# A kernel of attention and two expert layers: the squares of the last three row blocks behind the last score turn's rounding, and half of the put products behind the last rank

## The chip, the cores and the metric

The kernel runs on one core of a Trainium2 chip. The metric is device time in microseconds (us) of one execution. The engines are TensorE (PE, matrix products), VectorE (DVE), ScalarE (ACT), GpSimd (POOL) and SyncE (SP, which issues transfers). Each engine executes its own queue in the order in which the program gives it. An instruction that waits for another engine holds up everything behind it on its own.

## What is computed

Attention with hashed buckets runs over 2 x 8 heads, 768 positions, 64 columns. Its output, 1,536 rows of 512 columns, goes through two layers of eight experts each: the first sends every row to one expert, the second to two.

```python
def _attn_ref(q, k, v, proj):
    ...
    mask = q_bucket[:, :, :, None] == k_bucket[:, :, None, :]
    scores = np.where(mask, scale * np.matmul(q, k.transpose(0, 1, 3, 2)), -1e9)
    attn = np.exp(scores - np.max(scores, axis=-1, keepdims=True))
    ...
def _moe_ref(x, expert_emb, tau, w1, w2):
    xn = x / (np.linalg.norm(x, axis=-1, keepdims=True) + 1e-06)
    logits = xn @ en.T / tau
    expert_idx = np.argmax(logits, axis=1)
    probs = np.exp(logits - logits.max(-1, keepdims=True))
    ...
    h = np.maximum(x[mask] @ w1[e], 0.0)
    out[mask] = gate_w[mask, None] * (h @ w2[e])
```

The change touches the norm of the rows (`np.linalg.norm`), whose sum of squares ACT computes, and the order around it.

## The kernel before

**Stages.** Attention fills 0 to about 287 us of the trace, the first expert layer about 287 to 493, the second the rest. Products in full precision are split into a high and a low part (names ending in `h` and `l`).

**Attention.** There are 32 groups `g` (16 heads, two halves of the rows), each with three score turns `j`. A turn is: PE's scores (L597), DVE's maximum (L602), the scale of it `mxs` (L607, L608, mostly on POOL), ACT's exponential (L612). Six transposes per group follow (L620), each rounded on ACT (`eh`, L624) with its rest on DVE (`el`, L630), and the products with the values (L647, L648). A group ends with ACT's copy `os` (L652), PE's L657 and DVE's L671 and L673, which write the rows `xrow` (task `fo`).

**Routing.** The 1,536 rows lie in twelve blocks of 128, taken in four triples T0 = 0, 3, 6, 9. For each triple there are, in the names of the planner's tasks:
- `rsa`, three squares of the first 448 columns, and `rsb`, three of the last 64 (function `r1_sq`, L679 to L684, the instruction is at L683). Each adds up its squares with an accumulator read right behind it.
- `r7` and `rm`, the logits and the best expert `hot` on DVE (L692 to L695, L686 to L690); `rr0` and `rr`, the rank of every row among those of its expert on PE (L241, L243, then L249, L251).
- `rn`, the norm on POOL (L304 to L306); `rv`, its application (L309, L310); `re`, the exponential of the gate on ACT (L313); `rg`, the gate (L317 to L319).
- `rp`, the row's place (L264, L267); `ra`, three scatters from POOL to memory (L719); `ro`, the overflow arithmetic on POOL (L274 to L279); `rc`, the carry of the rank to the next triple (L255, L257).

**The first expert** doesn't read its rows back. For T0 = 6 and 9 they are put into place by products (`xo`, `x0_put`, L769) of the rounded rows (`xa` on ACT, L756, and their rest `xb` on POOL, L759) with one-hot tiles (`oh`, DVE, L741). The products for the columns d = 0, 1 go to a tile S, those for d = 2, 3 to a tile ET. ACT and DVE copy both to `xh` (L1036) and `xl` (L1043), and the expert's first product starts (L1056). In the experts, `hh` and `hl` (L1062, L1066) are the hidden rows, L1080 to L1082 the second product, `ys` (L1104) its copy on ACT, L1125 its transpose. Weights come by SP (L202), are split on ACT (L211) and DVE (L217), and stand in ACT's queue between these. The second expert's rows and their weights `meta` come back from memory by SP (L996, L991), after the scatters, with the weights behind them in SP's queue.

**What sets the order.** The routines are tasks of a list scheduler, `Plan`. `add(name, engine, duration, function, due, dependencies, use=, new=)` registers one. `plan.order()` sorts all tasks by the starts that it plans from durations, due times and dependencies, and the instructions are emitted in that order, so that a planned duration of one task can move any task on any engine. `use` and `new` name ring slots: `new` opens one, here `("rt", T0)`, the small tiles of a triple. The first scatter of T0 = 6 depends also on `("rn", 9)`, so that all six scatters of the last two triples stand behind the norm of the last one on POOL.

Of the kernel before, what the change touches and what calls it, by code (L numbers as in the profile page):

```python
# [9 lines left out]
F32 = mybir.dt.float32  # L10
# [11 lines left out]
N, D, E, F = NB * S, NHEAD * DH, 8, 1024  # L22
# [33 lines left out]
class Plan:  # L56
# [7 lines left out]
    def add(self, name, eng, dur, fn, due, deps=(), use=(), new=(), lat=0):  # L64
        self.steps[name] = (eng, dur, fn, due, tuple(deps), tuple(use) + tuple(new), tuple(new), lat)
# [66 lines left out]
def lsh_attention_moe_moe2_kernel(  # L132
# [252 lines left out]
    acon, rt, rows = ap("acon", 1), ap("rt", 2), ap("rows", 1)  # L385
# [291 lines left out]
    R1 = {}  # L677

    def r1_sq(T0, t, last):  # L679
        if t == 0 and not last:  # L680
            R1[T0] = dict(ss=rt.tile([128, 3, 2], F32, name="ss"))
        c = slice(D - DH, D) if last else slice(0, D - DH)
        nc.scalar.activation(sqj[:, c], xrow[:, T0 + t, c], AF.Square,  # L683
                             accum_out=R1[T0]["ss"][:, t, last:last + 1])  # L684
# [6 lines left out]

    def r1_pre(T0):  # L692

        l7 = R1[T0]["l7"] = rt.tile([128, 3, E], F32, name="l7")
        nc.vector.tensor_reduce(l7, LGP[:, T0:T0 + 3, :, :NHEAD - 1], axis=AX.X, op=OP.add)  # L695

    def r1_hot(T0):
# [81 lines left out]
    add = plan.add  # L779
    P = lambda f, *a, **k: (lambda: f(*a, **k))  # L780
# [5 lines left out]
    for h in range(HEADS):  # L786
        z = 12 * h
        due = lambda k, o=0.0: z + PR[k] + o
        if h > 1:
            add(("load", h), "SP", 1800, P(loads, h), due("load"), [("load", h - 1)] if h > 2 else [], lat=2200,  # L790
                new=[("qk", h), ("vr", h)])
# [117 lines left out]
    for i, g in enumerate((14, 15, 30, 31)):  # L909
        T0, z = 3 * i, 6.0 * g + 8.5 + (L1 if i < 2 else 0)  # L910
        zg = z if i < 2 else z + 8 if i == 2 else z + 4
        hot = [("fo", x) for x in range(g % 2 + 16 * (g // 16), g + 1, 2)]
        w = L2 if i < 2 else .1
        prev = [("rc", T0 - 3)] if T0 else []
        for t in range(3):
            add(("rsa", T0, t), "ACT", 560, P(r1_sq, T0, t, 0), z - 3 + w * t, hot[:-1] + ([("rsa", T0, t - 1)] if t else []),
                use=[("rt", T0)] if t else [], new=[] if t else [("rt", T0)])
            add(("rsb", T0, t), "ACT", 240, P(r1_sq, T0, t, 1), z + (w * t if i < 2 else 4), hot + [("rsa", T0, 2)] + [("th", 31, 5)] * (i == 2), use=[("rt", T0)])
        U = dict(use=[("rt", T0)])
        add(("r7", T0), "DVE", 260, P(r1_pre, T0), z - 3, hot[:-1] + [("rsa", T0, 0)], use=[("rt", T0)])  # L920
        add(("rm", T0), "DVE", 760, P(r1_top, T0), 191.5 if i == 2 else z, hot + [("r7", T0)], use=[("rt", T0)])
        add(("rr0", T0), "PE", 120, P(r1_rank0, T0), z - (0 if i < 2 else 1), prev + [("tr", 31, 5)] * (i == 2) + [("c3",), ("rm", T0) if i < 2 else ("fp", g)], new=[("ET", ("k", T0))])
        add(("rr", T0), "PE", 228, P(r1_rank, T0), z, [("rm", T0), ("rr0", T0)], use=[("ET", ("k", T0)), ("rt", T0)])
        add(("rq", T0), "DVE", 452, P(r1_hot, T0), zg, [("rm", T0)] + [("tl", 1, 31, 5)] * (i == 2), **U)
        add(("rp", T0), "DVE", 315, P(r1_pos, T0), zg, [("rr", T0), ("rq", T0)],
            use=[("ET", ("k", T0)), ("rt", T0)])
        add(("rn", T0), "POOL", 1325, P(lambda T0: gate1_norm(rt, R1[T0]["ss"], 3, R1[T0]), T0), zg,
            [("rsb", T0, t) for t in range(3)], **U)
        add(("rv", T0), "DVE", 309, P(lambda T0: gate1_scale(3, R1[T0]), T0), zg, [("rn", T0), ("rm", T0)], **U)
        add(("re", T0), "ACT", 113, P(lambda T0: gate1_exp(R1[T0]), T0), zg, [("rv", T0)], **U)  # L930
        add(("rg", T0), "DVE", 506, P(lambda T0: gate1_out(rt, 3, R1[T0], xrow[:, T0:T0 + 3, D]), T0), zg,
            [("re", T0)] + [("fo", 31)] * (i == 2), **U)
        for t in range(3):
            add(("ra", T0, t), "POOL", 1038, P(r1_scatter, T0, t), z + 1 + w * t, [("rp", T0), ("rg", T0)]
                + ([("ra", T0, t - 1)] if t else []) + [("in", len(inits) - 1)]
                + ([("rn", 9)] if (T0, t) == (6, RA) else []), **U)
        if i < 3:
            add(("rc", T0), "POOL", 699, P(lambda T0: rank_carry(rt, R1[T0]["hot"], 3, 1), T0), z + (0 if i < 3 else 2),
                [("rm", T0), ("rr0", T0)] + prev, **U)
        add(("ro", T0), "POOL", 1064, P(r1_over, T0), z + 9, [("rp", T0), ("ra", 9 if i > 1 else T0, 2)], **U)  # L940
        add(("rk", T0), "SP", 1500, P(r1_keep, T0), z + (3 if i < 3 else 0), hot)
# [5 lines left out]
    for i, T0 in enumerate((6, 9)):  # L947
# [13 lines left out]
                use=[("ET", ("k", T0)), ("rt", T0)] + ([("es", ("oh", T0))] if t else []), new=[] if t else [("es", ("oh", T0))])  # L961
        for d in range(4):
            add(("xo", T0, d), "PE", 650, P(x0_put, T0, d), z + 1.5 + 3 * (d // 2) + d * .1 if i else 197 + 2 * (d // 2) + .1 * d,
                [("xb", T0, d), ("oh", T0, 2), ("e0t", d)] + ([("xo", 6, d)] if i else [("fp", 31)]),
                use=[(("S", "x0"), ("ET", "x0"))[d // 2], ("es", ("oh", T0))])
    for f in plan.order():
        f()
# [641 lines left out]
```

## Time and profile before

| | |
|---|---|
| time before, median of 3 runs | 811.01 us (807.99 to 813.76) |
| profiled execution | 808.55 us, span 806.8 us |
| mean granted clock of TensorE | 0.991 of full speed |
| PE busy | 774.3 us (96%) |
| DVE busy | 583.6 us (72%) |
| ACT busy | 479.5 us (59%) |
| POOL busy | 382.3 us (47%) |

A row of a timeline gives the start in us from the start of the span, the length, the engine, the line of the kernel, the operation, the tile written and the tiles read, the shapes, and in square brackets how long the engine stood idle ahead of it and what ended that. PE is busy nearly all the time, so the stretches in which it isn't, and what is waited for there, are what to look at.

### The profile page before, as it was taken

Reading aid. Unit: us, or ns where it says so; the run is one execution under the profiler, and the core shown is the slowest. Engines: PE = TensorE matmul, PEld = TensorE weight load, DVE = VectorE, ACT = ScalarE, POOL = GpSimd, SP = SyncE. Lnnn points to the kernel's source line nnn. Section 1 sums busy time; section 2 is a strip of 40 time slices with the busy share of each in tenths; the row PEclk is TensorE's granted clock in tenths of the full one; section 3 lists DMA queues with packets and bytes.
Section 4 is the critical chain, followed back from the end, with each engine's and each line's share of the span. In section 5 each row is a group of like instructions: output and inputs, shape, how many; then the busy total and the mean of one; then the engine's idle time right before and its main releaser. Section 6 shows DMA issues by size and latency. Waiting matters only on the chain. (4 is left out here: it accounts for less than half of the span.)

```text
span 806.8 us, 14991 instructions
## 1 busy us (share of the span) xinstructions
PE 774.3 (96%) x5078; PEld 748.5 (93%) x5078; DVE 583.6 (72%) x1303; ACT 479.5 (59%) x1009; POOL 382.3 (47%) x669
## 2 busy tenths in 40 slices
PE   8999798998999999999999998999999999999995
PEld 6899787987999999999999998999999999999995
DVE  8999778999999868887787756684566475665511
ACT  6997777986888847556575544464353435354310
POOL 6655344557464260433123322108373745648474
PEclk9999989999999999999999999999999999999998
DMA  8999999664322158886677645765786776856332
GB/s 215 290 237 233 244 235 247 208 187 143 112 67 53 46 178 252 258 255 196 207 231 218 214 161 176 183 192 93 195 172 173 171 182 132 177 147 118 85 35 80
DMA packets 94076, 141.16 MB, mean 175 GB/s; under 512 B 26220, under 2 KB 58116, under 8 KB 93994
## 3 DMA queue, kind: packets, MB, share of 16 engines
q1 hardware_dynamic: 76730, 123.45, 55.2%
q0 software_dynamic: 17264, 16.70, 11.1%
q8 instruction: 42, 0.69, 0.4%
q14 instruction: 40, 0.33, 0.1%
HBM read 89.08 MB, written 36.06 MB: 155 GB/s over the span
## 5 line engine op out<-in xcount | busy, mean ns | idle before, releaser
L1264 POOL DMA_INDIRECT out_dram<-yo,idx x91 | 147.6, 1622 | 127.6 <-DVE yo L1261 102.0
L1056 PE MATMUL S<-xh,w0h 128*128 128x256 f32 (+1 forms) x512 | 165.0, 322 | 1.0 <-DVE hl L1066 1.0
L1057 PE MATMUL S<-xl,w0h 128*128 128x256 f32 (+1 forms) x512 | 161.4, 315 | 0.3 <-issue 0.3
L1058 PE MATMUL S<-xh,w0l 128*128 128x256 f32 (+1 forms) x512 | 161.7, 316 | 0.0
L1080 PE MATMUL ET<-hh,w1h 128*128 128x256 f32 (+2 forms) x504 | 158.5, 315 | 0.1
L1082 PE MATMUL ET<-hh,w1l 128*128 128x256 f32 (+2 forms) x504 | 158.2, 314 | 0.0
L1081 PE MATMUL ET<-hl,w1h 128*128 128x256 f32 (+2 forms) x504 | 157.8, 313 | 0.0
L1062 ACT ACTIVATE hh<-S 128x512 fp32r<-128x512 f32 (+1 forms) x64 | 46.8, 732 | 136.1 <-PE S L1058 130.1
L630 DVE TENSOR_TENSOR el<-ET,eh 128x384 fp32r<-128x384 f32 x192 | 102.0, 551 | 16.1 <-ACT eh L624 13.9
L612 ACT ACTIVATE es<-S,mxs 128x768 f32<-128x768 f32 x96 | 95.5, 995 | 15.7 <-POOL mxs L608 12.8
L620 PE MATMUL ET<-idf,es 128*128 128x128 f32 x576 | 92.1, 277 | 9.7 <-ACT es L612 7.1
L1066 DVE SCALAR_TENSOR_TENSOR hl<-S,hh 128x512 fp32r<-128x512 f32 (+1 forms) x64 | 54.5, 852 | 64.2 <-ACT hh L1062 62.3
L624 ACT ACTIVATE eh<-ET 128x384 fp32r<-128x384 f32 x192 | 89.7, 492 | 14.6 <-PE ET L620 11.3
L1056 PEld LDWEIGHTS S<-xh,w0h 128*128 128x128 f32 x512 | 96.3, 188 | 1.4 <-DVE hl L1066 1.2
L1057 PEld LDWEIGHTS S<-xl,w0h 128*128 128x128 f32 x512 | 96.4, 188 | 1.3 <-issue 0.5
L1058 PEld LDWEIGHTS S<-xh,w0l 128*128 128x128 f32 x512 | 96.2, 188 | 0.3
L1080 PEld LDWEIGHTS ET<-hh,w1h 128*128 128x128 f32 x504 | 94.9, 188 | 1.1 <-ACT ys L1104 0.7
L1081 PEld LDWEIGHTS ET<-hl,w1h 128*128 128x128 f32 x504 | 94.8, 188 | 0.7
L602 DVE TENSOR_REDUCE mxs<-S 128x1 f32<-128x768 f32 x96 | 91.5, 953 | 5.1 <-PE S L597 4.0
L1082 PEld LDWEIGHTS ET<-hh,w1l 128*128 128x128 f32 x504 | 94.7, 188 | 0.3
L620 PEld LDWEIGHTS ET<-idf,es 128*128 128x128 f32 x576 | 71.9, 142 | 20.6 <-ACT es L612 8.1
L217 DVE TENSOR_TENSOR w1l<-wraw,w1h 128x512 fp32r<-128x512 f32 x128 | 81.9, 681 | 11.8 <-ACT w1h L211 11.8
(257 smaller groups left out, 1474.7 us busy)
## 6 DMA issues: line engine op xcount, KB each, us to landing
wraw<-in_w1a_dram SPq DMA_DIRECT2D x32, 512.0 KB
wraw<-in_w2a_dram SPq DMA_DIRECT2D x32, 512.0 KB
wraw<-in_w1b_dram SPq DMA_DIRECT2D x32, 512.0 KB
wraw<-in_w2b_dram SPq DMA_DIRECT2D x32, 512.0 KB
xs<-zrow SPq DMA_DIRECT2D x26, 260.5 KB
xr<-xs SPq DMA_DIRECT2D x28, 208.0 KB
qk<-in_qk_dram SPq DMA_DIRECT2D x15, 384.0 KB
xs<-zrow SPq DMA_DIRECT2D x16, 261.0 KB
```

Of the source, the lines that this page charges most:

```text
L602: nc.vector.tensor_reduce(MX[(3 * g + j) % 9][:, 0:1], SC[g, j][:, :, :384], axis=AX.XY, op=OP.max, negate=True)
L612: nc.scalar.activation(ES[g, j].rearrange("p (a b) -> p a b", a=2), SC[g, j][:, :, :384], AF.Exp, bias=mx[:, 2:3], scale=mx[:, 1:2], accum ...
L620: nc.tensor.transpose(T[:, j * 128:j * 128 + 128], ES[g, j][:, kb * 128:kb * 128 + 128], idf)
L624: nc.scalar.activation(EH[g, kb], ET[g, kb], AF.Copy)
L630: nc.vector.tensor_tensor(EL[g, kb], ET[g, kb], EH[g, kb], op=OP.subtract)
L1056: nc.tensor.matmul(o, wH[n][:, fs], xh, start=kd == 0, stop=False)
L1057: nc.tensor.matmul(o, wH[n][:, fs], xl, start=False, stop=False)
L1058: nc.tensor.matmul(o, wL[n][:, fs], xh, start=False, stop=kd == 3)
L1080: nc.tensor.matmul(P, wH[n][:, ws], hh, start=f == 0, stop=False)
L1081: nc.tensor.matmul(P, wH[n][:, ws], hl_, start=False, stop=False)
L1082: nc.tensor.matmul(P, wL[n][:, ws], hh, start=False, stop=f == 7)
L1264: s = nc.gpsimd.indirect_dma_start(out=out.rearrange("n (a c) -> (n a) c", a=4), out_offset=bass.IndirectOffsetOnAxis(ap=IDX[e][:, b:b + 1 ...
```

## The change

Planned durations of all squares go from 560 and 240 to 850 and 370. The long squares of the last triple, T0 = 9, depend now on the rounding of the last score turn's transpose, `("th", 31, 5)`, and on the last rounding of rows, `("xa", 9, 3)`, and are due 3 later instead of 3 earlier. The logits `r7` of that triple no longer wait for its first square and open its ring slot. The put products of T0 = 6 for d = 2 and 3 depend on the last rank, `("rr", 9)`.

```diff
--- before.py
+++ after.py
@@ -678,7 +678,7 @@
 
     def r1_sq(T0, t, last):
         if t == 0 and not last:
-            R1[T0] = dict(ss=rt.tile([128, 3, 2], F32, name="ss"))
+            R1.setdefault(T0, {})["ss"] = rt.tile([128, 3, 2], F32, name="ss")
         c = slice(D - DH, D) if last else slice(0, D - DH)
         nc.scalar.activation(sqj[:, c], xrow[:, T0 + t, c], AF.Square,
                              accum_out=R1[T0]["ss"][:, t, last:last + 1])
@@ -691,7 +691,7 @@
 
     def r1_pre(T0):
 
-        l7 = R1[T0]["l7"] = rt.tile([128, 3, E], F32, name="l7")
+        l7 = R1.setdefault(T0, {})["l7"] = rt.tile([128, 3, E], F32, name="l7")
         nc.vector.tensor_reduce(l7, LGP[:, T0:T0 + 3, :, :NHEAD - 1], axis=AX.X, op=OP.add)
 
     def r1_hot(T0):
@@ -913,11 +913,11 @@
         w = L2 if i < 2 else .1
         prev = [("rc", T0 - 3)] if T0 else []
         for t in range(3):
-            add(("rsa", T0, t), "ACT", 560, P(r1_sq, T0, t, 0), z - 3 + w * t, hot[:-1] + ([("rsa", T0, t - 1)] if t else []),
-                use=[("rt", T0)] if t else [], new=[] if t else [("rt", T0)])
-            add(("rsb", T0, t), "ACT", 240, P(r1_sq, T0, t, 1), z + (w * t if i < 2 else 4), hot + [("rsa", T0, 2)] + [("th", 31, 5)] * (i == 2), use=[("rt", T0)])
+            add(("rsa", T0, t), "ACT", 850, P(r1_sq, T0, t, 0), z + (3 if i == 3 else -3) + w * t, hot[:-1] + [("th", 31, 5), ("xa", 9, 3)] * (i == 3) + ([("rsa", T0, t - 1)] if t else []),
+                use=[("rt", T0)] if t or i == 3 else [], new=[] if t or i == 3 else [("rt", T0)])
+            add(("rsb", T0, t), "ACT", 370, P(r1_sq, T0, t, 1), z + (w * t if i < 2 else 4), hot + [("rsa", T0, 2)] + [("th", 31, 5)] * (i == 2), use=[("rt", T0)])
         U = dict(use=[("rt", T0)])
-        add(("r7", T0), "DVE", 260, P(r1_pre, T0), z - 3, hot[:-1] + [("rsa", T0, 0)], use=[("rt", T0)])
+        add(("r7", T0), "DVE", 260, P(r1_pre, T0), z - 3, hot[:-1] + [("rsa", T0, 0)] * (i < 3), **({"new": [("rt", T0)]} if i == 3 else {"use": [("rt", T0)]}))
         add(("rm", T0), "DVE", 760, P(r1_top, T0), 191.5 if i == 2 else z, hot + [("r7", T0)], use=[("rt", T0)])
         add(("rr0", T0), "PE", 120, P(r1_rank0, T0), z - (0 if i < 2 else 1), prev + [("tr", 31, 5)] * (i == 2) + [("c3",), ("rm", T0) if i < 2 else ("fp", g)], new=[("ET", ("k", T0))])
         add(("rr", T0), "PE", 228, P(r1_rank, T0), z, [("rm", T0), ("rr0", T0)], use=[("ET", ("k", T0)), ("rt", T0)])
@@ -961,7 +961,7 @@
                 use=[("ET", ("k", T0)), ("rt", T0)] + ([("es", ("oh", T0))] if t else []), new=[] if t else [("es", ("oh", T0))])
         for d in range(4):
             add(("xo", T0, d), "PE", 650, P(x0_put, T0, d), z + 1.5 + 3 * (d // 2) + d * .1 if i else 197 + 2 * (d // 2) + .1 * d,
-                [("xb", T0, d), ("oh", T0, 2), ("e0t", d)] + ([("xo", 6, d)] if i else [("fp", 31)]),
+                [("xb", T0, d), ("oh", T0, 2), ("e0t", d)] + ([("xo", 6, d)] if i else [("fp", 31)] + [("rr", 9)] * (d > 1)),
                 use=[(("S", "x0"), ("ET", "x0"))[d // 2], ("es", ("oh", T0))])
     for f in plan.order():
         f()
```

ACT's queue at the end of attention (L624 rounds the last score turns' transposes, L652 is `os`, L756 `xa`, L683 the squares, L313 the gate's exponential, L1036 `xh`), before:

```order
L683 ACTIVATE sqj,ss<-xrow 128x448
L652 ACTIVATE os<-O 128x384
L624 ACTIVATE eh<-ET 128x384 x2
L683 ACTIVATE sqj,ss<-xrow 128x448 x2
L624 ACTIVATE eh<-ET 128x384
L756 ACTIVATE lx<-xrow 128x384
L624 ACTIVATE eh<-ET 128x384
L683 ACTIVATE sqj,ss<-xrow 128x64 x3
L652 ACTIVATE os<-O 128x384
L756 ACTIVATE es<-xrow 128x384
L683 ACTIVATE sqj,ss<-xrow 128x64 x3
L313 ACTIVATE z<-z 128x24 x2
```

and the same place now:

```order
L652 ACTIVATE os<-O 128x384
L624 ACTIVATE eh<-ET 128x384 x2
L756 ACTIVATE lx<-xrow 128x384
L624 ACTIVATE eh<-ET 128x384
L683 ACTIVATE sqj,ss<-xrow 128x64 x3
L652 ACTIVATE os<-O 128x384
L756 ACTIVATE es<-xrow 128x384
L683 ACTIVATE sqj,ss<-xrow 128x448
L313 ACTIVATE z<-z 128x24
L683 ACTIVATE sqj,ss<-xrow 128x448 x2
L683 ACTIVATE sqj,ss<-xrow 128x64 x3
L313 ACTIVATE z<-z 128x24
```

The three long squares of T0 = 9 have moved from among the copies of the last turns to behind the rounding L756, and the exponential of T0 = 6 now stands between them.

PE's queue at the put products (L243 starts the last rank, L249 and L251 finish it, L769 are the puts), the difference:

```order
 L243 MATMUL ET<-base,idr 128x24
 L769 MATMUL S<-es,qk 128x256 x12
-L769 MATMUL ET<-es,qk 128x256 x6
 L249 MATMUL ET<-hot,onr 128x16
 L249 MATMUL ET<-hot,onr 128x8
 L251 MATMUL ET<-hot,upr 128x24
+L769 MATMUL ET<-es,qk 128x256 x6
 L769 MATMUL ET<-es,lx 128x256 x6
```

The last rank stands ahead of the first six products into ET instead of behind them.

POOL's queue at the scatters of T0 = 0 (L661 is a small operation of a group's end), before:

```order
L661 TENSOR_SCALAR sm<-sm 128x3
L719 DMA xs_58<-xrow,pi 12288x522 x2
L607 TENSOR_SCALAR mxs<-mxs 128x1
L608 TENSOR_TENSOR mxs<-mxs 128x1
L719 DMA xs_58<-xrow,pi 12288x522
L274 CAST ov<-pi 128x3
```

and now, where L304 to L306 are the norm of T0 = 3:

```order
L661 TENSOR_SCALAR sm<-sm 128x3
L304 TENSOR_TENSOR nr<-ss 128x3
L305 TENSOR_TENSOR nr<-nr,half 128x3
L306 TENSOR_SCALAR nr<-nr 128x3
L607 TENSOR_SCALAR mxs<-mxs 128x1
L608 TENSOR_TENSOR mxs<-mxs 128x1
L719 DMA xs_58<-xrow,pi 12288x522
L607 TENSOR_SCALAR mxs<-mxs 128x1
L608 TENSOR_TENSOR mxs<-mxs 128x1
L719 DMA xs_58<-xrow,pi 12288x522 x2
L274 CAST ov<-pi 128x3
```

One scatter goes now ahead of the middle pair of `mxs` and two behind it, in front of the overflow arithmetic, and the norm of T0 = 3 stands here instead of further up. Behind the overflow arithmetic the next `mxs` pair follows in both.

## Rows read from the trace of the kernel before

**Rows 1.** Busy time by stretch: bounds, length, PE, PEld, DVE, ACT, POOL, PEclk, DMA, GB/s.
```profile
100.00:110.00 10.00, 9.55 (x47) 9.19 (x48) 6.98 (x15) 7.51 (x19) 6.28 (x17) 0.69 0.99 225
...
180.00:190.00 10.00, 8.83 (x57) 7.86 (x55) 9.52 (x31) 6.22 (x12) 8.35 (x22) 1.00 0.37 134
190.00:200.00 10.00, 8.50 (x52) 6.94 (x53) 8.69 (x22) 6.47 (x16) 6.82 (x17) 1.00 0.69 199
...
270.00:287.00 17.00, 16.71 (x130) 16.07 (x129) 13.90 (x66) 11.83 (x41) 7.73 (x16) 1.00 0.28 106
287.00:300.00 13.00, 11.67 (x95) 11.26 (x95) 8.25 (x15) 6.50 (x13) 10.03 (x29) 1.00 0.49 151
300.00:315.00 15.00, 14.97 (x124) 14.55 (x123) 11.19 (x25) 10.15 (x21) 1.41 (x3) 1.00 0.96 285
315.00:490.00 175.00, 174.91 (x1468) 173.90 (x1467) 132.51 (x388) 105.78 (x227) 53.38 (x106) 1.00 0.69 213
```

**Rows 2.** Timeline of PE around 187 us.
```profile
187.62 0.62 PE L597 MATMUL S<-ka,qa 96*128 96x384 f32 x2 [0.47 <-ACT es L612]
```

**Rows 3.** Timeline of POOL at the scatters of row block 0.
```profile
181.54 0.99 POOL L719 DMA_INDIRECT xs<-xrow,pi  x1 [0.30 <-issue]
182.54 0.30 POOL L607 TENSOR_SCALAR mxs<-mxs 128x1 f32<-128x1 f32 x1
...
183.63 1.08 POOL L719 DMA_INDIRECT xs<-xrow,pi  x1 [0.51 <-issue]
...
185.94 0.24 POOL L607 TENSOR_SCALAR mxs<-mxs 128x1 f32<-128x1 f32 x1
```

**Rows 4.** Timeline of ACT from the last rounding to the third `ys`.
```profile
281.21 0.53 ACT L756 ACTIVATE es<-xrow 128x384 fp32r<-128x384 f32 x1 [1.73 <-DVE xrow L673]
281.64 0.24 ACT L683 ACTIVATE sqj<-xrow 128x64 f32<-128x64 f32 x1
...
282.39 0.26 ACT L683 ACTIVATE sqj<-xrow 128x64 f32<-128x64 f32 x1
...
282.80 0.22 ACT L313 ACTIVATE z<-z 128x24 f32<-128x24 f32 x1
285.51 0.22 ACT L313 ACTIVATE z<-z 128x24 f32<-128x24 f32 x1 [2.48 <-DVE z L310]
...
303.93 1.16 ACT L211 ACTIVATE w0h<-wraw 128x512 fp32r<-128x512 f32 x2 [2.38 <-DMA wraw<-in_w1a_dram]
...
310.28 0.38 ACT L1104 ACTIVATE ys<-ET 128x256 f32<-128x256 f32 x1
```

**Rows 5.** Timeline of POOL: last norm, first and last of six scatters.
```profile
282.81 0.20 POOL L304 TENSOR_TENSOR nr<-ss 128x3 f32<-128x3 f32 x1
...
284.06 0.24 POOL L306 TENSOR_SCALAR nr<-nr 128x3 f32<-128x3 f32 x1
284.78 1.13 POOL L719 DMA_INDIRECT xs<-xrow,pi  x1 [0.48 <-DVE es L741]
...
291.55 1.50 POOL L719 DMA_INDIRECT xs<-xrow,pi  x1 [0.30 <-issue]
```

**Rows 6.** SP, 278 to 312 us: timeline, then its longest wait (total, times, longest).
```profile
295.38 0.88 SPq L996 DMA_DIRECT2D meta<-xs  x2
...
SPq L996 <- DMA xs<-xrow,pi: 13.4, 1, 13.4
```

**Rows 7.** Timeline of PE: six put products, and the matmul that needs the third `ys`.
```profile
282.49 0.88 PE L769 MATMUL ET<-es,qk 128*128 128x256 f32 x6
...
310.71 0.39 PE L1080 MATMUL ET<-hh,w1h 128*128 128x256 f32 x1
```

**Rows 8.** Timeline of ACT: the last two long squares.
```profile
275.23 0.63 ACT L683 ACTIVATE sqj<-xrow 128x448 f32<-128x448 f32 x1
...
275.97 0.58 ACT L683 ACTIVATE sqj<-xrow 128x448 f32<-128x448 f32 x1
```

**Rows 9.** ACT's groups by line: the function table.
```profile
L149 ACT ACT_TABLE_LOAD x1 | 1.3, 1283 | 0.8 <-PEq L1598 0.8
```

## Prediction

> **What bounds the kernel now.** I read the page first: PE is busy 774.3 of 806.8 us, so a change can matter only where PE stands still, or where it makes PE stand still. The busy time by stretch then says where that is [rows 1]. From 180 to 200 us PE is busy 8.83 + 8.50 = 17.33 of 20 us, from 270 to 287 it lacks 0.29 us, from 287 to 300 it lacks 1.33, from 300 to 315 it lacks 0.03, and from 315 to 490 it lacks 0.09 of 175 us. The last number decides how the rest is read: whatever PE loses or wins before 315 us is carried whole to the end of the first expert layer, since nothing between could take it up. The timelines of the single engines then tell what stands behind each loss.
>
> In the middle (180 to 200) PE waits for the exponential of a score turn, L612 on ACT [rows 2], and that waits for `mxs`, L607 and L608 on POOL, which is queued behind POOL's scatters and its overflow arithmetic [rows 3]: the third scatter of row block 0 starts at 183.63, and the next `mxs` starts only at 185.94, 2.31 us later.
>
> At the end of attention PE is full, but the first expert hangs on a long chain that starts on ACT and POOL. I follow it in the order of the program. The rounding `xa`(9,3) (L756) starts on ACT at 281.21 [rows 4]. Three 64-column squares follow, then POOL's norm of row blocks 9 to 11 ends at 284.06 + 0.24 = 284.30, and the first of six scatters starts at 284.78 [rows 5]: all six stand behind this norm in POOL's queue. The last ends at 291.55 + 1.50 = 293.05. SP, which waits 13.4 us for them, reads `meta` back at 295.38 and only then issues the next expert's rows and weights [rows 6]. ACT waits 2.38 us for these and splits them at 303.93, and behind that split, in ACT's own order, stand the copies `ys` (L1104) of the first expert. The third starts at 310.28 and lasts 0.38, so ends at 310.66; PE's matmul that needs it starts at 310.71 [rows 4, 7]. The slack of the whole chain is thus 0.05 us, although PE shows no wait there.
>
> **The change, part by part.**
>
> *Nine squares' worth of planning numbers, 560 to 850 and 240 to 370.* The work is the same: a 448-column square follows the one before by 275.97 - 275.23 = 0.74 us, a 64-column one by (282.39 - 281.64) / 2 = 0.38 [rows 4, 8]. So the instructions cost nothing more. Only the order moves, and the place where this meets a wait is POOL from 175 to 200 us. For row block 0 the order had scatter x2, `mxs`, scatter, overflow, `mxs`; it now has scatter, `mxs`, scatter x2, overflow, `mxs`. The block in front of the last `mxs` grows by one scatter: 182.54 - 181.54 = 1.00 and the gap of 0.30 that stands ahead of it [rows 3], 1.3 us on top of 2.31. Against this the first `mxs` has one scatter less in front. The norm of row block 3 also moves behind a carry and in front of an `mxs`, which costs it 284.30 - 282.81 = 1.49 us by the norm of the tail [rows 5]. What PE loses here now is bounded by its idle time, 2.67 us over both stretches [rows 1]. Erasing it all is the lower end, -2.7. Losing as much again is the upper, +2.7. Two things speak for a loss (a longer block; a norm in front of an `mxs`), one for a gain. An `mxs` that is late is mostly taken up by the work that PE has in stock: the 2.31 us block cost it 0.47 [rows 2]. I take +0.5, the price of one more such block.
>
> *The three 448-column squares of row blocks 9 to 11 go behind the rounding.* Before, they stood ahead of copies that the last score turn needs, the last two at 275.23 and 275.97 [rows 8]. So some 3 x 0.74 = 2.2 us of ACT time come free there. PE lacks only 0.29 us between 270 and 287 [rows 1], so the chain to the rounding comes forward by less. I take 0.7 us, between 0.3 (the visible idle time) and 1.0 (about half the ACT time, an estimate). The rounding then starts at 280.5.
>
> Behind it the squares are on the chain. Before: from the start of the rounding to the end of the norm 284.30 - 281.21 = 3.09 us. After, counted from its start: the rounding 0.43 (281.64 - 281.21), the first square 0.74, which is over at 1.17; then the exponential of row blocks 6 to 8, which waits for DVE and so stays at 282.80 - 281.21 = 1.59; with its 0.22 that gives 1.81; two squares to 3.29; three short squares to 4.43; and from there to the norm's end what it takes now, 284.30 - 282.77 = 1.53. Sum 5.96, which is 2.87 more than 3.09. Less the 0.7 won above, the norm ends 2.2 us later. The bounds are 1.9 (1.0 won) and 2.6 (0.3 won).
>
> What is queued behind it: on POOL the six scatters, first at about 286.9 instead of 284.78; on ACT the second exponential, 285.51 now [rows 4], and `xh` right behind it, which go to about 287.1 and later, so that the first expert's first matmuls have their operands about a microsecond later. That is not the last wait. The scatters' 2.2 us go on through SP's `meta`, the weights and ACT's split (303.93 to 306.1) to the third `ys`, which ends at 312.9 instead of 310.66. PE stands 2.2 - 0.05 = 2.15 us for it, in pieces in front of the turns L1125 and the matmuls behind them. I enter **+2.1**.
>
> *Rank of the last triple behind the first twelve put products.* PE executes the same rows. The rank stands one group of six products earlier in PE's queue (0.88 us long [rows 7]), and DVE's one-hot tile `oh`, which needs it, stands ahead of three gate operations. The puts would then end up to 0.9 us earlier. This is worth nothing while `xh` stands behind the second exponential and the chain above ends last. If that cover were gone it would be worth -0.9.
>
> *A ring slot opened by `r7` rather than by the square, and a dictionary filled in another way:* no instruction, 0.
>
> **Sum.** 808.55 (span 806.8 and 1.75 around it) + 2.1 + 0.5 = 811.15 on the scale of the profiled execution. The median of the runs shown, 811.01, lies 2.46 above that execution, and the runs go from 807.99 to 813.76. On the median's scale the sum is 813.6. I put the forecast between, at **812**.
>
> **A rule against the change.** The change puts an exponential between squares of the same triple. In this trace ACT loads a function table once in all, 1283 ns [rows 9], although squares and exponentials already alternate on it. So the alternation costs nothing, and this stays out of the sum. The Trainium skill, page "ScalarE: Activation LUTs", section "Table sets: the hidden batching unit", tells to batch activations by table set, since each switch to another set costs about 2.7 us; going by that alone the sum would get some 5 us more (an estimate from that page). The row bears it out only in that one set serves both.
>
> **Rivals.**
> - *The late norm is hidden.* If the scatters' landing is not what SP's reads end on, or the weights are late for another reason, the +2.1 falls away: 809.1. Against it: SP's wait of 13.4 us ends on the scatters [rows 6], and the slack is 0.05. Chance 0.15.
> - *Faster: the middle wins.* POOL's new order lets every `mxs` go in time and the whole 2.67 us there come back. It decides from a gain of 2.1 us on. With the tail's loss that gives 808.0; with the tail hidden as well, and the puts' 0.9, 805.0. For it: the first `mxs` has a scatter less in front. Against it: the longer block. Chance 0.17.
> - *The middle loses.* Each of the two longer POOL blocks costs PE a further microsecond or more, up to the same 2.7 again: 813.4. Chance 0.15.
> - *TensorE's clock falls.* The granted clock was 0.69 in 100 to 110 us, directly after PE had stood still, and 1.00 in all stretches around the change [rows 1]. A 10 us stretch at 0.69 costs 3.1 us. If the longer standstill at about 287 or those at 307 to 312 bring the lower of the two levels (1.2 GHz), the time is 811.15 + 3.1 = 814.3. Against it: 1.33 us idle in 287 to 300 did not. Chance 0.06. The Trainium skill's page "TensorE: Matmul & The Clock Gate", section "Why this matters for your kernels", warns of idle gaps between bursts of matmuls for that reason; the first stretch agrees with it.
>
> The forecast itself keeps 0.47. On the mean of both scales (add 1.2) the cases lie at 806 to 809, 810, 812, 814.6 and 815.5. The range that leaves out at most two in ten goes from 808 to 816; the forecast's own, with its bounds, from 810.5 to 814. About one per cent, 8.1 us, is what a measurement of this kernel can tell from no change. No case reaches that far in either direction; what is left is the unknown and the spread of the runs: faster 0.03, within 0.94, slower 0.03.
>
> **What would show it.** In the trace of the changed kernel: the rounding at about 280.5, the norm's end at about 286.5, the first scatter at about 286.9, SP's `meta` at about 297.5, the split at about 306, and a new PE idle time of about 2 us between 306 and 313, all relative to the kernel's own middle. In 180 to 200 PE should be busy within 1.5 us of 17.33. I am wrong if the scatters come no later, if PE shows no wait at 306 to 313 although they do, or if the stretch before 200 us moves by more than the tail does.

## The result and the profile after

The changed kernel takes 816.32 us (median of 9 runs, 812.96 to 818.74). The kernel before takes 811.66 us over its 9 runs (807.99 to 813.76). The ratio is 1.0062, with a 95% interval of 1.0037 to 1.0086: slower by 0.6%, about 4.7 us. I had forecast 812, a range from 808 to 816 and a rise of 2.6 us: the sign was right and the size was not.

| | before | after |
|---|---|---|
| profiled execution, us | 808.55 | 817.89 |
| span, us | 806.8 | 815.9 |
| mean granted clock of TensorE | 0.991 | 0.980 |
| PE busy, us | 774.3 | 777.6 |

The two profiled executions lie 9.3 us apart, twice the distance of the medians. So I compare inside them. The 81st exponential of the score turns starts at 234.97 us before and 236.91 after. From the 65th to the 89th the distance of the two executions is constant (1.92 to 1.95 us), so I take 1.94 off the times of after wherever I compare a single time. Of this 1.94 us, 1.3 are there already at the 45th exponential (136.8 us before), ahead of the first difference in the order of any engine, and 0.6 come between it and the 73rd (214.7 us before).

Busy time of the changed kernel by stretch (columns as in [rows 1]):

```profile
180.00:190.00 10.00, 9.03 (x64) 8.51 (x61) 9.62 (x29) 5.95 (x14) 7.50 (x19) 1.00 0.59 186
190.00:200.00 10.00, 8.30 (x50) 6.64 (x50) 8.27 (x23) 6.78 (x16) 8.03 (x19) 1.00 0.53 154
270.00:287.00 17.00, 16.91 (x131) 16.20 (x130) 14.51 (x61) 13.20 (x42) 4.92 (x13) 1.00 0.25 93
287.00:300.00 13.00, 11.99 (x99) 11.59 (x98) 8.63 (x21) 7.41 (x18) 10.11 (x18) 1.00 0.33 126
300.00:315.00 15.00, 11.42 (x85) 11.02 (x85) 7.09 (x14) 6.23 (x13) 3.52 (x16) 0.92 0.81 221
315.00:490.00 175.00, 174.64 (x1460) 173.23 (x1459) 132.87 (x391) 104.43 (x223) 53.51 (x106) 1.00 0.69 215
```

From 180 to 200 us PE is as busy as before (9.03 + 8.30 = 17.33, as in [rows 1]), but these windows hold other pieces of work than before, since this execution is 1.3 us or more late by then. Between the same two exponentials, the 45th and the 73rd, the middle takes 78.60 us where it took 77.97. The stretch from 300 to 315 has lost 3.55 us of PE time (14.97 to 11.42), and its granted clock is 0.92 instead of 1.00. Behind it everything is full again up to 490 us, as before. Where the second layer starts there is one more difference, in the clock. The kernel before, then the changed one:

```profile
490.00:500.00 10.00, 6.97 (x50) 6.46 (x50) 7.21 (x31) 3.89 (x11) 2.63 (x4) 0.94 0.78 248
500.00:510.00 10.00, 10.00 (x52) 9.89 (x51) 5.37 (x10) 5.53 (x11) 6.21 (x10) 0.89 0.34 91
```

```profile
490.00:500.00 10.00, 8.93 (x76) 8.74 (x74) 6.05 (x14) 6.92 (x17) 2.08 (x5) 1.00 0.70 176
500.00:510.00 10.00, 8.05 (x41) 7.66 (x40) 5.54 (x27) 2.60 (x9) 3.88 (x5) 0.69 0.54 212
```

The granted clock is at the lower level (1.2 GHz) for 3.4 us before (498.8 to 502.2) and for 6.8 us after (503.9 to 510.7), and from the 29th to the 41st hidden rows `hh` (L1062) of the experts the kernel takes 114.9 us before and 116.3 after, with 3.0 us of PE idle time in both. I come back to this below.

The larger loss lies where the chain of the prediction ends. PE, timeline of the changed kernel:

```profile
310.93 0.73 PE L1125 MATMUL ET<-iw,ys 128*128 128x144 f32 x4 [3.09 <-ACT ys L1104]
312.15 0.38 PE L1080 MATMUL ET<-hh,w1h 128*128 128x256 f32 x1 [0.49 <-ACT ys L1104]
```

PE waits 3.09 + 0.49 = 3.58 us for the copies `ys`, where it showed no wait before [rows 7]. And here is the clock behind that wait, in a stretch cut to its bounds:

```profile
312.70:316.10 3.40, 3.40 (x18) 3.40 (x17) 2.94 (x5) 2.60 (x5) 1.44 (x3) 0.50 0.75 194
316.10:320.00 3.90, 3.90 (x33) 3.70 (x32) 2.92 (x9) 2.26 (x5) 0.00 (x0) 1.00 0.77 274
```

The granted clock is 0.50, the lower level (1.2 GHz), for 3.4 us. PE counts as fully busy in them, yet ends 18 products against 33 in the next 3.9 us.

The chain that leads there, ACT's timeline of the changed kernel:

```profile
278.41 0.49 ACT L624 ACTIVATE eh<-ET 128x384 fp32r<-128x384 f32 x1 [0.96 <-DVE xrow L673]
...
281.06 0.49 ACT L652 ACTIVATE os<-O 128x384 f32<-128x384 f32 x1 [0.37 <-PE O L648]
283.08 0.52 ACT L756 ACTIVATE es<-xrow 128x384 fp32r<-128x384 f32 x1 [1.53 <-DVE xrow L673]
283.51 0.56 ACT L683 ACTIVATE sqj<-xrow 128x448 f32<-128x448 f32 x1
...
284.68 0.22 ACT L313 ACTIVATE z<-z 128x24 f32<-128x24 f32 x1 [0.51 <-DVE z L310]
...
286.82 0.26 ACT L683 ACTIVATE sqj<-xrow 128x64 f32<-128x64 f32 x1
...
289.19 0.22 ACT L313 ACTIVATE z<-z 128x24 f32<-128x24 f32 x1 [2.02 <-DVE z L310]
...
309.37 1.15 ACT L211 ACTIVATE w0h<-wraw 128x512 fp32r<-128x512 f32 x2 [6.60 <-DMA wraw<-in_w1a_dram]
310.43 0.36 ACT L1104 ACTIVATE ys<-ET 128x256 f32<-128x256 f32 x1
```

The squares stand behind the rounding at 283.08 as the order said. The first copy `ys` comes right behind the split of the second expert's weights, for which ACT waits 6.60 us (2.38 before [rows 4]). POOL's timeline, norm and scatters, and SP's read of `meta`:

```profile
287.25 0.20 POOL L304 TENSOR_TENSOR nr<-ss 128x3 f32<-128x3 f32 x1 [2.64 <-ACT sqj L683]
...
288.50 0.23 POOL L306 TENSOR_SCALAR nr<-nr 128x3 f32<-128x3 f32 x1
289.22 1.13 POOL L719 DMA_INDIRECT xs<-xrow,pi  x1 [0.49 <-DVE z L310]
...
293.33 1.50 POOL L719 DMA_INDIRECT xs<-xrow,pi  x1 [0.30 <-issue]
295.14 1.50 POOL L719 DMA_INDIRECT xs<-xrow,pi  x1 [0.31 <-issue]
296.94 0.97 POOL L719 DMA_INDIRECT xs<-xrow,pi  x1 [0.30 <-issue]
```

```profile
300.66 0.88 SPq L996 DMA_DIRECT2D meta<-xs  x2
```

POOL waits 2.64 us for the squares, the first scatter starts at 289.22 (284.78 before [rows 5]) and `meta` is read at 300.66 (295.38 before [rows 6]).

### The profile page after: what moved, and what is told of

It reads as the page before. It is cut to its first block, busy times and chain, and to the rows that moved or that the text cites. A ratio compares the mean times of both kernels' runs of the same rounds, so it can differ in the third digit from the quotient of the medians.

```text
span 815.9 us, 14986 instructions
## 1 busy us (share of the span) xinstructions
PE 777.6 (95%) x5078; PEld 751.8 (92%) x5078; DVE 583.9 (72%) x1303; ACT 479.8 (59%) x1009; POOL 381.4 (47%) x669
## 5 line engine op out<-in xcount | busy, mean ns | idle before, releaser
L1080 PE MATMUL ET<-hh,w1h 128*128 128x256 f32 (+2 forms) x504 | 159.3, 316 | 0.5 <-ACT ys L1104 0.5
L1062 ACT ACTIVATE hh<-S 128x512 fp32r<-128x512 f32 (+1 forms) x64 | 46.8, 732 | 134.4 <-PE S L1058 133.4
L620 PE MATMUL ET<-idf,es 128*128 128x128 f32 x576 | 93.2, 279 | 11.7 <-ACT es L612 7.7
L624 ACT ACTIVATE eh<-ET 128x384 fp32r<-128x384 f32 x192 | 89.6, 491 | 14.8 <-PE ET L620 11.7
L1080 PEld LDWEIGHTS ET<-hh,w1h 128*128 128x128 f32 x504 | 95.6, 190 | 2.2 <-ACT ys L1104 1.9
L620 PEld LDWEIGHTS ET<-idf,es 128*128 128x128 f32 x576 | 72.4, 143 | 23.2 <-ACT es L612 8.9
L217 DVE TENSOR_TENSOR w1l<-wraw,w1h 128x512 fp32r<-128x512 f32 x128 | 81.9, 682 | 10.8 <-ACT w1h L211 10.8
```

The costliest lines, as they stand in the source:

```text
L620: nc.tensor.transpose(T[:, j * 128:j * 128 + 128], ES[g, j][:, kb * 128:kb * 128 + 128], idf)
L624: nc.scalar.activation(EH[g, kb], ET[g, kb], AF.Copy)
L1080: nc.tensor.matmul(P, wH[n][:, ws], hh, start=f == 0, stop=False)
```

## Experiments

The theory to test is the chain: late squares, late norm, six late scatters, late weights of the second expert, and `ys` behind them on ACT, with a stretch of low clock on top. Its rivals: the order of the middle; something at the start; the first expert's late rows (`xh` behind the second exponential). The ratios below are to the kernel before in the same comparison.

| kernel | median, us | ratio (95% interval) |
|---|---|---|
| changed kernel | 816.32 | 1.0062 (1.0037 to 1.0086) |
| late squares alone | 816.17 | 1.0063 (1.0045 to 1.0081) |
| changed, without the late squares | 812.52 | 1.0018 (0.9996 to 1.0040) |
| earlier rank alone | 811.18 | 0.9998 (0.9975 to 1.0020) |
| changed, weights ahead of `meta` | 816.56 | 1.0084 (1.0059 to 1.0108) |
| changed, `ys` ahead of the weights | 810.62 | 1.0000 (0.9979 to 1.0020) |
| before, `ys` ahead of the weights | 809.00 | 0.9988 (0.9969 to 1.0007) |
| changed, PE's wait filled | 813.92 | 1.0044 (1.0023 to 1.0065) |
| changed, squares in ACT's gap | 816.11 | 1.0072 (1.0046 to 1.0098) |
| before, `ys` ahead and earlier rank | 808.63 | 0.9978 (0.9950 to 1.0006) |

And the chain in their traces, in us counted from the start of the rounding L756 of the last rows in the same trace. L211 is the first split of the second expert's weights on ACT, L1125 the first transpose of `ys` on PE. "13th `hh`" is the start of the thirteenth L1062 of the experts, which tells what the whole chain has cost by then. The last column is the length of the stretch from the 29th to the 41st `hh`, where the second layer starts.

| kernel | norm ends | last scatter ends | L211 starts | L1125 starts | 13th `hh` | 29th to 41st |
|---|---|---|---|---|---|---|
| before | 3.1 | 11.8 | 22.7 | 25.3 | 87.0 | 114.9 |
| changed | 5.6 | 14.8 | 26.3 | 27.9 | 91.9 | 116.3 |
| late squares alone | 5.0 | 14.0 | 25.2 | 26.8 | 91.2 | 116.4 |
| changed, without the late squares | 3.1 | 11.7 | 22.0 | 25.2 | 87.3 | 114.8 |
| earlier rank alone | 3.3 | 12.1 | 23.2 | 24.7 | 88.1 | 114.9 |
| changed, weights ahead of `meta` | 5.6 | 14.5 | 15.2 | 29.6 | 92.5 | 116.3 |
| changed, `ys` ahead | 5.6 | 14.8 | 26.3 | 24.6 | 86.7 | 114.9 |
| before, `ys` ahead | 3.1 | 11.7 | 25.0 | 23.4 | 85.9 | 115.5 |
| changed, PE's wait filled | 5.6 | 14.8 | 26.4 | 27.9 | 91.1 | 114.9 |
| changed, squares in ACT's gap | 3.3 | 13.2 | 25.2 | 26.7 | 90.8 | 116.2 |
| before, `ys` ahead and earlier rank | 3.3 | 12.6 | 24.7 | 23.1 | 85.8 | 114.8 |

**The late squares alone.** The second piece of the change on the kernel before; planned durations and puts as before.

```diff
-add(("rsa", T0, t), "ACT", 560, ..., z - 3 + w * t, hot[:-1] + ...
+add(("rsa", T0, t), "ACT", 560, ..., z + (3 if i == 3 else -3) + w * t,
+    hot[:-1] + [("th", 31, 5), ("xa", 9, 3)] * (i == 3) + ...
```

> The kernel before with the late squares of the last triple alone: the old planned durations stay, and the put products keep the old place of the last rank. Tail theory: the whole loss of the changed kernel (811.7 to 816.3) comes from the six scatters standing behind the late norm, through the second expert's weights to the copies ys, plus a stretch of low TensorE clock that the new standstill brings. Then this kernel is at 815 to 816.5, with a PE wait of 2 to 3.5 us on ys (L1104) between 306 and 313 us. Rival, the order of the middle: then it is at 811 to 812.5, because the middle is as before. Rival, the start: then it is at 815 to 817 with a tail like that of before.

Measured 816.17 us, the whole loss, with the middle in the old order. PE's waits of this kernel between 270 and 330 us (total, times, longest):

```profile
PE ET L1125 <- ACT ys L1104: 2.1, 1, 2.1
PE ET L1080 <- ACT ys L1104: 0.9, 2, 0.5
```

Together 3.0 us, inside what was expected. The granted clock stays at 1.00 behind these waits, and still the thirteenth `hh` starts 4.2 us later than before: the larger part of the loss does not need the clock. Where the second layer starts, the clock is at the lower level for 6.8 us here too, and the stretch there takes 1.5 us more than before, so it is not shown that the whole loss would come without the clock. The rivals of the middle and of the start fall.

**The changed kernel without the late squares.** New planned durations and the earlier rank, nothing else.

```diff
-add(("rsa", T0, t), "ACT", 850, ..., z + (3 if i == 3 else -3) + w * t, hot[:-1] + [("th", 31, 5), ("xa", 9, 3)] * (i == 3) + ...
+add(("rsa", T0, t), "ACT", 850, ..., z - 3 + w * t, hot[:-1] + ...
```

> The changed kernel without the late squares: new planned durations and the earlier last rank, but the long squares of the last triple among the copies as before. Tail theory: 811.5 to 813, with no PE wait on ys between 306 and 313 us, and the middle some 0.5 us longer than before. Rival, the order of the middle: 815 to 816.5.

Measured 812.52 us. The interval reaches from no change to 0.4%, so the reordered middle costs between nothing and 3 us by the clock on the wall. The traces are finer. From the 45th to the 73rd exponential of the score turns the five traces with the old order take 77.9 to 78.2 us, mean 78.0, and the six with the new one 78.3 to 78.7, mean 78.55. That is +0.55, and the two groups do not overlap.

**The earlier rank alone.**

```diff
-[("xb", T0, d), ("oh", T0, 2), ("e0t", d)] + ([("xo", 6, d)] if i else [("fp", 31)]),
+[("xb", T0, d), ("oh", T0, 2), ("e0t", d)] + ([("xo", 6, d)] if i else [("fp", 31)] + [("rr", 9)] * (d > 1)),
```

> The kernel before with the last rank ahead of the first six put products into ET, nothing else moved but DVE's one-hot tile. Tail theory: the puts end 0.5 to 1 us earlier, and this is lost again at the copies ys, so 811 to 812. Rival, the puts are on the path: 810.7 to 811.

Measured 811.18 us, no difference. The puts end 0.3 us earlier than before (against the 81st exponential), less than the 0.5 to 1 that I had expected, and PE waits at the transposes, where the trace of before showed no wait:

```profile
304.55 0.73 PE L1125 MATMUL ET<-iw,ys 128*128 128x144 f32 x4 [0.32 <-ACT ys L1104]
305.77 0.38 PE L1080 MATMUL ET<-hh,w1h 128*128 128x256 f32 x1 [0.49 <-ACT ys L1104]
```

So the chain through `ys` can bind with the squares and ACT's order of the kernel before as well.

**Weights ahead of `meta`.** The second expert's first weights no longer wait in SP's queue for the scatters.

```diff
-add(("wr", n), "SP", 1700, P(wload, n), z - 14, [("wr", n - 1) if n > 8 else ("xl", 1)] + ...
+add(("wr", n), "SP", 1700, P(wload, n), z - 14, ([("wr", n - 1)] if n > 8 else []) + ...
```

> The changed kernel, where the second expert's first weights no longer wait in SP's queue for the read of meta, which waits for the scatters. Late norm and late scatters stay. Tail theory: ACT's split of these weights and so the copies ys come without waiting, the PE wait on ys at 306 to 313 us and the low clock behind it are gone, 811 to 813. Rival, PE's wait comes from something else in the tail (the late xh): 815 to 817.

Measured 816.56 us, the rival's number. But its trace shows that the experiment did not do what it was to do: the planner, given earlier weights, put the next piece of weights in front of `ys`, and that piece stands behind `meta`. ACT of this kernel:

```profile
308.75 0.63 ACT L211 ACTIVATE w1h<-wraw 128x512 fp32r<-128x512 f32 x1 [4.06 <-DMA wraw<-in_w2a_dram]
309.29 0.36 ACT L1104 ACTIVATE ys<-ET 128x256 f32<-128x256 f32 x1
```

The wait was moved to another transfer behind the same scatters. It decides nothing between the theories.

**`ys` ahead of the weights, on the changed kernel.** Two dependencies put the first two copies ahead of the split and of the second expert's `xh`. Norm, scatters and SP's queue stay late. The planner also moves some of the later splits and copies of the second expert.

```diff
 add(("wh", n, k), "ACT", 520, P(wsplit_h, n, 2, k), z + k, ...
-    ([("wh", n, 0)] if k else ([("wh", n - 1, 1)] if n > 4 else [])),
+    ([("yc", 0, 1)] if (n, k) == (8, 0) else []) + ([("wh", n, 0)] if k else ([("wh", n - 1, 1)] if n > 4 else [])),
 ...
-... else [("xt", key, dp)],
+... else [("xt", key, dp)] + [("yc", 0, 1)] * (key == 1),
```

> The changed kernel, where in ACT's queue the first two copies ys of the first expert stand ahead of the split of the second expert's weights and of the rounding xh of its rows; SP's queue up to these weights, the norm and the scatters stay late. Chain theory (the late norm costs through ys standing behind the late weights): the PE wait of 3.1 us ahead of L1125 goes, no low clock follows, some 0.5 to 1.5 us of waiting remain further on, because the second expert's weights themselves are late: 812 to 814. Rival, the loss comes from the late first products (xh behind the second exponential): 815.5 to 817, wait or no wait on ys.

Measured 810.62 us, ratio 1.0000: the whole loss is gone, more than I expected. ACT's timeline:

```profile
305.22 0.39 ACT L1104 ACTIVATE ys<-ET 128x256 f32<-128x256 f32 x1 [3.68 <-PE ET L1082]
306.77 0.38 ACT L1104 ACTIVATE ys<-ET 128x256 f32<-128x256 f32 x1 [1.17 <-DMA wraw<-in_w1a_dram]
307.05 1.14 ACT L1036 ACTIVATE xh<-xs 128x512 fp32r<-128x512 f32 x2
308.09 2.18 ACT L211 ACTIVATE w0h<-wraw 128x512 fp32r<-128x512 f32 x4
```

The operand of both copies is PE's product, which ends just ahead of each (the transfer named in the second row landed at about the same time, and the copy doesn't need it). The split of the weights starts just as late (26.3 us behind the rounding, in both), now without a wait for the transfer, which landed about 1.5 us earlier than in the changed kernel but still 2 us later than before. PE has no wait on the weights. `xh` is as late as in the changed kernel, with PE waits of 0.56 + 0.42 us, so the rival of the late rows falls as the cause of the loss.

**`ys` ahead of the weights, on the kernel before.** The same edit.

> The kernel before with the same order of ys, weights and xh on ACT. Chain theory: ys is just in time there, with 0.05 us of slack, so nothing is won at ys: 810.5 to 811.5. If the slack is negative in most executions, 809.5 to 810.5.

Measured 809.00 us, ratio 0.9988 with an interval that holds 1. In the trace PE starts L1125 23.4 us behind the rounding instead of 25.3, without a wait. Between 287 and 300 us, where the order is that of before, PE of this kernel is full:

```profile
287.00:300.00 13.00, 13.00 (x111) 13.00 (x111) 8.27 (x15) 7.09 (x14) 9.97 (x28) 1.00 0.48 148
```

In the profile of before it lacked 1.33 us there [rows 1], since ACT had stood still ahead of the first `hh` of that expert, and the view does not name what for. ACT of the kernel before:

```profile
293.55 0.60 ACT L1062 ACTIVATE hh<-S 128x512 fp32r<-128x512 f32 x1 [1.43 <-remote]
```

By the trace's records of signals between engines, the product that this `hh` needs is over 9.9 us behind the rounding and PE's signal comes at 12.3, while in the kernel with `ys` ahead the product ends and the signal comes at 9.2. (The recorded ends of products are modelled.) Why it came late is open. The hold-up is not of that one execution: the kernels of the first four experiments have one at the same place, with PE standing still for 0.25 to 1.65 us, and the changed kernel and the last five don't have it. Without it PE reaches L1125 about 1.9 us earlier than in the trace of before, so these 1.9 us are not what the edit won. The two kernels with `ys` ahead, neither with the hold-up, show in their traces what the late rows cost: L1125 at 24.6 against 23.4 us behind the rounding, 1.2 us. Their medians, 810.62 against 809.00 us, also hold the reordered middle, and their intervals overlap. In the changed kernel the wait for `ys` covers the late rows.

**PE's wait filled.** 22 products of no use stand ahead of the first transpose.

```diff
+def fill():
+    P = psp.tile([128, 512], F32, name="O", bufs=1)
+    for i in range(22):
+        nc.tensor.matmul(P[:, :256], wH[4][:, :128], XH[0, 0][:, :256], start=True, stop=True)
 ...
+add(("fill",), "PE", 10, fill, Z[0] + 1.3 * 11 - .05, [("m2", 0, 1, 1)], new=[("O", "fill")])
```

> The changed kernel with 22 more products of 256 columns on PE, of no use, in front of the first transpose L1125 (L1131 here): they fill most of the 3.1 us in which PE waits for ys there. The wait itself stays. Clock theory: 1.5 us of the loss come from the 3.4 us at half clock that follow this standstill; the granted clock between 300 and 320 us is then 1.00 and the time 814.3 to 815.3. Rival, the low clock costs nothing, since the copies ys set the pace there anyhow: 816 to 816.6.

Busy time from 300 to 320 us, and PE's timeline (L1131 here is L1125 of the others, L1086 is L1080):

```profile
300.00:320.00 20.00, 18.23 (x148) 17.62 (x148) 12.17 (x27) 10.65 (x23) 2.22 (x11) 1.00 0.95 262
```

```profile
305.54 2.79 PE L1051 MATMUL O<-xh,w1h 128*128 128x256 f32 x22
308.86 0.73 PE L1131 MATMUL ET<-iw,ys 128*128 128x144 f32 x4 [0.54 <-ACT ys L1110]
310.08 0.39 PE L1086 MATMUL ET<-hh,w1h 128*128 128x256 f32 x1 [0.49 <-ACT ys L1110]
314.44 0.38 PE L1086 MATMUL ET<-hh,w1h 128*128 128x256 f32 x1 [0.74 <-ACT ys L1110]
```

The clock stays at 1.00 and the wait for `ys` ends at the same place (27.9 us behind the rounding in both). From there to the thirteenth `hh` of the experts the kernel takes 63.2 us, against 64.1 in the changed kernel. So the low clock cost 0.9 us in this pair of traces, not the 1.5 that I had expected: PE at full clock has to wait 0.74 us for the third `ys`. That part of what full clock gives is taken back by waits shows in the late squares alone as well, which need 64.4 us for the same stretch at full clock, with 2.0 us of PE idle time in it (1.5 here, 0.9 in the changed kernel). The time, 813.92 us, lies 2.4 below the changed kernel, but the two intervals overlap, so the size by the clock on the wall stays open. In this trace the clock is low for only 3.4 us where the second layer starts, 1.4 us less time there than in the changed kernel, so the 2.4 need not come from the filled wait alone.

**Squares in ACT's gap.** Only the first of the two dependencies.

```diff
-hot[:-1] + [("th", 31, 5), ("xa", 9, 3)] * (i == 3)
+hot[:-1] + [("th", 31, 5)] * (i == 3)
```

> The changed kernel without the second of the two new dependencies: the long squares of the last triple wait only for the last score turn's rounding and not for the rounding of the rows, so that ACT does them in the time in which it waits for DVE ahead of that rounding. Chain theory: the norm ends as early as in the kernel before or up to 0.5 us later, and the time is 811 to 812.5. Rival, the squares now hold up the copy os or the rounding: 813 to 816.

Measured 816.11 us: a miss. The norm does end early, 3.3 us behind the rounding. But the rounding itself comes 0.6 us later against the 81st exponential, held up by squares, and then the scatters take longer. POOL, SP and PE:

```profile
285.30 0.23 POOL L306 TENSOR_SCALAR nr<-nr 128x3 f32<-128x3 f32 x1
286.02 1.13 POOL L719 DMA_INDIRECT xs<-xrow,pi  x1 [0.49 <-DVE z L310]
...
291.56 1.51 POOL L719 DMA_INDIRECT xs<-xrow,pi  x1 [0.30 <-issue]
293.38 2.10 POOL L719 DMA_INDIRECT xs<-xrow,pi  x1 [0.30 <-issue]
```

```profile
299.40 0.88 SPq L996 DMA_DIRECT2D meta<-xs  x2
```

```profile
308.98 1.30 PE L1125 MATMUL ET<-iw,ys 128*128 128x144 f32 x4 [4.10 <-ACT ys L1104]
```

From the first scatter to the end of the last it is 9.46 us here (8.27 before), and from there to the read of `meta` 3.92 (2.33 before). PE starts the first expert's products 5.3 us behind the rounding (6.7 in the changed kernel), comes early to L1125, waits 4.10 us and then runs at the lower clock level. So an early norm alone does not bring the time back: by this trace the second expert's rows and weights, and `ys` with them, follow the last scatter and not the norm. Why the last one landed so late stays open: this is one trace.

**`ys` ahead and the earlier rank, on the kernel before.** Both edits shown above.

> The kernel before with ys ahead of the second expert's weights and rows on ACT, and with the last rank ahead of the first six put products into ET. With ys free, the microsecond that the earlier rank won in the puts and lost again at ys (experiment with the rank alone) should now stay: some 1 us under the kernel with ys ahead alone, 807.5 to 809.5, ratio about 0.996 to 0.998. Rival, the puts are not on the path even then: as with ys ahead alone, ratio 0.9985 to 0.9995.

Measured 808.63 us, the lowest median of all, ratio 0.9978 (0.9950 to 1.0006). The trace has L1125 23.1 us behind the rounding, 0.3 earlier than with `ys` ahead alone, as much as the puts win and not the microsecond of the expectation. That this version beats the kernel before is likely and not shown.

## Why the prediction was wrong

*What bounds the kernel.* Right in the chain: the late squares alone bring the loss, without them it goes, and the experiment with `ys` ahead takes away the last link and the loss with it. The links between, from the scatters to the weights, were read from the traces; the one experiment on them, weights ahead of `meta`, failed. Wrong in one number. I read "the slack of the whole chain is thus 0.05 us" off the end of `ys` and the start of PE's next matmul [rows 4, 7]. The two met because PE had itself been held up by 1.33 us, in a row that I had read [rows 1] without asking whether every execution has it. The experiment with the earlier rank shows PE waiting at `ys` with squares and ACT's order as before. So PE came to L1125 earlier than I had it, in spite of the late `xh`: 310.93 - 3.09 - 1.94 = 305.90 on the time of before, against 306.46. The visible wait became 3.58 us where I had entered 2.15. Against the trace of before this makes PE 2.6 us late at L1125 (27.9 against 25.3 us behind the rounding), since before PE had lost its 1.33 us on the way.

*ACT's freed time.* I let the rounding come forward by 0.7 us. It came forward by 283.08 - 1.94 = 281.14 against 281.21 [rows 4], which is nothing. About half of the 2.2 us turned up as ACT waits in the same place, 0.96, 0.37 and 1.53 us in the rows above where one of 1.73 had stood [rows 4]; the rounding is released by DVE's `xrow` in both. The lower bound that I gave, 0.3, was too high as well.

*The squares behind the rounding.* From the rounding to the end of the norm I had 5.96 us; it is 288.73 - 283.08 = 5.65. The difference to before, 2.87 forecast, is 5.65 - 3.09 = 2.56. With nothing won ahead of it, the norm ends 2.5 us late, where I had 2.2: inside the bounds.

*The same delay all along the chain.* I carried 2.2 us unchanged from the norm to `ys`. It grew. On the time of before the first scatter is late by 289.22 - 1.94 - 284.78 = 2.5, the end of the last by 2.9, `meta` by 3.3, and the split of the weights by 309.37 - 1.94 - 303.93 = 3.5 us. The six scatters take 8.69 us instead of 8.27, two of them 1.50 us long instead of one. The long ones run beside DVE's split of weights (below); that this is why is not shown.

*The clock.* I had this as a rival with a chance of 0.06. It happened in the changed kernel: 3.4 us at the lower level behind the 3.09 us standstill, at a cost of 0.9 us in the trace. My argument against it, that 1.33 us idle in 287 to 300 had not lowered the clock, compared 1.33 us in two pieces with one wait of 3.09. The Trainium skill, page "TensorE: Matmul & The Clock Gate", section "Why this matters for your kernels", warns of idle gaps between bursts of matmuls; the trace agrees with it at 312.7 us. A place that I had not thought of is the start of the second layer, with 6.8 us at the lower level instead of 3.4, and 1.4 us more time. In the table above the stretch there takes 116.2 us and more in the four kernels in which PE waits over 2 us for `ys`, and 115.5 or less in the seven others, the one with the wait filled among them. That the wait brings it, 190 us later, is not shown.

*The middle.* +0.5 forecast, +0.55 in the traces. The longer block is there, as the order said, POOL and PE of the changed kernel:

```profile
186.76 0.98 POOL L719 DMA_INDIRECT xs<-xrow,pi  x1 [0.30 <-issue]
...
188.94 0.24 POOL L607 TENSOR_SCALAR mxs<-mxs 128x1 f32<-128x1 f32 x1
```

```profile
190.63 0.61 PE L597 MATMUL S<-ka,qa 96*128 96x384 f32 x2 [1.60 <-ACT es L612]
```

PE waits 1.60 us behind it, where it waited 0.47 [rows 2] and, one turn later, 0.93. PE of the kernel before:

```profile
190.43 0.62 PE L597 MATMUL S<-ka,qa 96*128 96x384 f32 x2 [0.93 <-ACT es L612]
```

So the block itself costs some 0.2 us, not the 0.5 that I had priced it at. The rest of the 0.55 lies elsewhere between the two exponentials, and that the sum came out at the forecast is in part luck.

*The earlier rank and the table.* Worth nothing while `ys` ends last: right. In the puts it is 0.3 us where I had 0.9. No further load of a function table, and an exponential of 0.22 us among the squares, as before.

*The forecast itself.* The sum on the scale of the medians was 813.6, and I set the forecast between the two scales at 812. On the median of before over nine runs the sum, +2.6, gives 814.3. The step that failed is the size of the tail's term, +2.1. In the traces the thirteenth `hh` of the changed kernel starts 4.9 us later behind the rounding than before. Some 0.8 of this is the low clock (91.9 against 91.1 us with PE's wait filled), which stood in the sum at nothing. The other 4.1 are the chain: 2.67 up to the first transpose, and 1.46 behind it, where PE stands still for 1.5 us with the wait filled and stood still for 0.1 us before. I had carried one delay of 2.2 us to one place; it had grown to 3.5 at the split, and the copies and splits behind it held PE up again. With the middle and the start of the second layer the changed trace loses 6.7 us against before from the 45th exponential to the 41st `hh`, more than the 4.7 us of the medians. So these are sizes of one pair of executions, and how the 4.7 us divide stays open.

## What to carry to other kernels

An operand that arrives just as its engine gets there is no proof that the chain has slack: the engine may have been late for another reason, which not every execution has, so look for an earlier wait on it that the profile does not explain. Bound a stretch by the same two instructions in both traces, not by the same times: windows of fixed time showed no change in the middle, and the stretch between two exponentials showed +0.55 us. On an engine that executes in order, the cheapest cure is often at the end of the chain: here two dependencies that let a short copy go ahead of a late weight took back all that a norm 2.5 us late had cost against the kernel before. And a delay handed along a chain of transfers need not be handed along unchanged: here 2.5 us at the norm were 3.5 at the split of the weights.

## What the hardware showed that I had not expected

A scatter on POOL (L719, 128 rows) takes longer beside DVE's split of weights (L217). Of the 66 scatters at the end of attention in the eleven traces, every one that takes over 1.2 us (1.21 to 2.10) overlaps L217 by 0.65 us or more, and none that overlaps by less takes over 1.13. Overlap alone does not suffice: some that run wholly beside it take 1.04 to 1.18. That DVE is the cause was not tried. The Trainium skill, page "DMA: Bandwidth & Descriptors", section "SWDGE vs HWDGE vs iDMA", says that the descriptors of such transfers are written by POOL into memory that DVE can lock POOL out of in one of its modes, which would fit; no run here shows in which mode L217 runs.

The lower clock level did not follow every wait for `ys`. After 2.14, 0.49 and 0.38 us, in the kernel with the late squares alone, the granted clock stayed at 1.00. After 3.09 and 0.49 us, in the changed kernel, it fell to 0.50 for 3.4 us, and after 3.15 and 0.49 us, in the kernel with the weights ahead of `meta`, it did the same. With 4.10 us, in the kernel with the squares in ACT's gap, it was at 0.50 for 6.8 us, from 307.1 us on, while PE was still waiting.
